# Loading w_out two rows to a partition, with w1, w2 and w3 read in column pairs

## The chip, the cores and the metric

One core of one Trainium2 chip runs the whole program. The metric is the device time of one execution in microseconds, lower being better. The core has five engines that run side by side, each taking its own instructions strictly in its own order: TensorE (matmuls, shown as PE, with its weight loads as PEld), VectorE (DVE), ScalarE (ACT), GpSimd (POOL) and SyncE (SP). Engines wait for each other, and for transfers, by semaphores.

## The reference

The inputs are q, k, v of shape (8, 8, 576, 64), phi of shape (8, 8, 576, 32), three matrices w1, w2, w3 of shape (512, 768), and w_out of shape (768, 512), all float32. Attention goes over 32 memory slots; its result, 4608 tokens of 512 features, goes through a maxout layer:

```python
a = exp(phi - max(phi, axis=2)); a = a / sum(a, axis=2)
k_m = einsum('bhsm,bhsd->bhmd', a, k)
v_m = einsum('bhsm,bhsd->bhmd', a, v)
attn = softmax(q @ k_m.T / sqrt(64))
x = (attn @ v_m).transpose(0, 2, 1, 3).reshape(4608, 512)
h = maximum(maximum(x @ w1, x @ w2), x @ w3)
out = h @ w_out
```

## The kernel before

All matmuls take bfloat16. The kernel never forms x. For each batch it multiplies the values of the memory slots into the weights ("folds" them), so that attention weights times folded weights give the hidden layer directly. The maxout is rewritten: the hidden layer is max(x(w1 - w3), x(w2 - w3), 0) + x w3, and the last term goes past the maximum straight to the output through w3 @ w_out, which is computed once.

The weights lie in SBUF as follows. `w_sb` holds w1, w2 and w3 in one tile: on partition p, for each j of four, row j*128 + p of w1, of w2 and of w3, each with 768 columns. `w12` is a view of it with the 1536 columns of w1 and w2 in one row. `wo_sb` holds w_out, six rows of 512 columns on each partition. `w3T` holds w3 transposed, and `w3o` the product w3 @ w_out.

The order of the work is written out by hand, as a string of short names in `kernel`'s list at the end, and no scheduler changes it. Each name issues one step for one batch (`D1@0` is step D1 for batch 0). What the framework adds are the semaphore waits: it records which addresses each instruction reads and writes, and lets the later of two that overlap wait for the earlier. The steps that matter here:

- `Y2`, `Y3`, `Y0`, `Y1` (in this order) load w3, w_out, w1 and w2 on POOL's queue, with a cast from float32 to bfloat16 on the way (`load_w`, L118, and `load_wo`, L125). The loads of k, v, phi and q (L99, L95, L112) go on the same queue, and are served in its order.
- `W0@0` to `W2@0` transpose w3 on TensorE: 24 transposes of 128 x 128 (`w3_t`, L202), which VectorE copies into `w3T` (L194). `O0@0` to `O3@0` multiply by w_out (`w3_o`, L225). `Z` steps are matmuls on zeros to keep TensorE running (L168).
- `D0` to `D4` are folds (`fold`, L494): matmuls of the 64-row, 32-column form, eight side by side, with 512 or 256 columns of w1 or w2 streaming through. For batch 0 w3 has not been subtracted yet, so the fold runs a second pass with w3 and negated values (`kvtn`). There `D1` has columns 512 to 768 of `w12` (the end of w1), `D0` columns 0 to 512 (w1), `D2` columns 768 to 1024 and `D4` columns 1024 to 1536 (both w2). In later batches `D0`, `D1`, `D2` take 512 columns each. `D3` folds `w3o`.
- `V0@0`, `V1@0`, `V2@0`, `V4@0` subtract w3 from the same column ranges of `w12`, in place, on VectorE (`w_diff`, L244), after the folds of batch 0 have read them.
- `F0` to `F11` are the hidden layer (`ffn1`, L520), even ones with w1 and odd ones with w2; ScalarE and VectorE take the results out of PSUM (L188, L192, L533). `P`, `p` and `T` form the output (L582, L567, L623), which SP stores.
- `S` is the attention score (L387), whose moving operand is every second bfloat16 of the transposed q (`Q`, L367).

Around the change the order by hand reads, for batch 0: `... R1 W0 Y3 W1 W2 H1 H3 Y0 Z6 O0 X1 X0 Y1 O1 L1@1 B1 N1 L0@1 O2 L3@1 K1 L2@1 O3 D1 D0 D3 F10 F8 V0 F4 V1 F0 F6 L2@2 F2 D2 V2 D4 L1@2 p1 L0@2 F3 F1 F11 ...`. A name on one engine does not hold up another engine's names, save through a semaphore.

Of the kernel before, what the change touches and what calls it, by code (L numbers as in the profile page):

```python
# [15 lines left out]
def kernel(  # L16
# [12 lines left out]
    nc = tc.nc  # L29
# [3 lines left out]
    P = 128  # L33
# [38 lines left out]
    w_sb = const.tile([P, NP, 3, DF], BF16, name="w_sb")  # L72
    w3T = const.tile([P, FT, NP, P], BF16, name="w3T")
    wo_sb = const.tile([P, FT, DM], BF16, name="wo_sb")
# [47 lines left out]
    ident = const.tile([P, P], BF16, name="ident")  # L122

    def load_wo():
        nc.gpsimd.dma_start(out=wo_sb, in_=moe_w_out.rearrange("(t p) c -> p t c", p=P))  # L125

    gate = const.tile([1, 2], BF16, name="gate")

# [28 lines left out]
    def one_bank():  # L157
        return psum[:, int(next(banks))]

    def two_banks():  # L160
        i = int(next(banks))
        return psum[:, i : i + 2]
# [12 lines left out]
    def evacuate(kind, n, how, out_, in_, relu=False):  # L175

        swap = "!" in how
        if "^" in how:
            first = "" if EVAC[kind][n] == "a" else "!"
            second = "!" if EVAC[kind][n] == "a" else ""  # L180
            x = 1 if kind == "D" and swap else 0
            evacuate(kind, n, first, out_[:, x], in_[:, x], relu)
            evacuate(kind, n, second, out_[:, 1 - x], in_[:, 1 - x], relu)
            return

        if (EVAC[kind][n] == "a") != swap:
            if relu:
                nc.scalar.activation(out=out_, in_=in_, func=AF.Relu)  # L188
            else:
                nc.scalar.copy(out=out_, in_=in_)  # L190
        elif relu:
            nc.vector.tensor_scalar_max(out=out_, in0=in_, scalar1=0.0)  # L192
        else:
            nc.vector.tensor_copy(out=out_, in_=in_)  # L194

    def w3_t(f2, swap):

        pt = one_bank().bitcast(BF16).rearrange("p (i j n) -> p i j n", i=2, j=NP)
        for i in range(2):
            f = 2 * f2 + i  # L200
            for j in range(NP):
                nc.tensor.transpose(  # L202
                    pt[:, i, j, :], w_sb[:, j, 2, f * P : (f + 1) * P], ident
                )
        evacuate("W", f2, swap, w3T[:, 2 * f2 : 2 * f2 + 2], pt)

# [31 lines left out]
    def columns(b, n):  # L238
        return FIRST[n] if b == 0 else (n * BANK, (n + 1) * BANK)
# [238 lines left out]
    def fold(b, n, swap):  # L478

        s = st[b]  # L480
        lo, hi = (0, DM) if n == 3 else columns(b, n)
        if n == 3:
            wp3s[b] = quad.tile([P, NG, DM], BF16, name="wp3")
        elif b not in wps:
            wps[b] = work.tile([P, NG, 2 * DF], BF16, name="wp")
        ps = two_banks()
        terms = [(s["kvt"][:, 0], w3o[:, :, lo:hi] if n == 3 else w12[:, :, lo:hi])]
        if b == 0 and n != 3:
            terms.append((s["kvtn"], w_sb[:, :, 2, lo % DF : lo % DF + hi - lo]))
        for i, (lhs, rhs) in enumerate(terms):  # L490
            for j in range(NP):
                for a in range(NG):
                    r = slice(HP * a, HP * (a + 1))
                    nc.tensor.matmul(  # L494
                        ps[M * j : M * (j + 1), a, 0 : hi - lo],
                        lhsT=lhs[r, M * j : M * (j + 1)],
                        rhs=rhs[r, j, :],
                        start=(i == 0),
                        stop=(i == len(terms) - 1),
                        tile_position=(HP * a, M * j),  # L500
                    )
        evacuate(
            "D", n, swap, wp3s[b] if n == 3 else wps[b][:, :, lo:hi], ps[:, :, 0 : hi - lo]
        )
# [141 lines left out]
    def issue(b, n, swap):  # L646
# [3 lines left out]
            "I": lambda: [make_identity(nc, ident)]  # L650
            + [nc.gpsimd.memset(x[:, :, :, 2 * D : 2 * D + 1], 1.0) for x in kvrs],
            "Y": lambda: load_w(i) if i < 3 else load_wo(),
            "L": lambda: load_ph(b) if i == 0 else load_q(b) if i == 3 else load_kv(b, i - 1),
            "H": lambda: load_kv(b, i % 2, halves[i // 2]),
# [13 lines left out]
            "M": lambda: ones_sum(b, i),  # L668
            "R": lambda: ones_rec(b, i),
            "D": lambda: fold(b, i, swap),  # L670
            "F": lambda: ffn1(b, i, swap),
            "P": lambda: ffn2_hidden(b, i, range(HEAD)),
            "p": lambda: ffn2_slots(b, i),
            "J": lambda: w3_o_head(i),
            "T": lambda: ffn2(b, i, swap),
            "W": lambda: w3_t(i, swap),
            "O": lambda: w3_o(i, swap),
            "V": lambda: w_diff(i),
# [5 lines left out]
    for w in """  # L684
# [24 lines left out]
        n, b = w.rstrip("!^").split("@")  # L709
# [31 lines left out]
```

## Time and profile before

| | us |
|---|---|
| median of 3 runs | 162.5 (162.21 to 162.69) |
| the profiled execution | 162.81 |
| its span, first to last instruction | 161.0 |
| TensorE busy | 153.0 (95%) |
| VectorE busy | 114.0 (71%) |
| ScalarE busy | 97.0 (60%) |
| GpSimd busy | 81.8 (51%) |

The span is what the profile's timeline covers; the rest of the time lies around it. A busy time is a share of the whole span, over stages with different limits: what one stage waits for is read from the waits and the timeline of that stage. In the lines of a timeline the columns are the start in us, the time taken, the engine, the line of the kernel, the operation, what it writes and reads, and how many such instructions are merged; in brackets is the idle time before, and what ended it. TensorE's granted clock is listed as 1.00 in all slices.

### The profile page before, as it was taken

How to read it: one execution, taken by the hardware profiler on the slowest of the kernel's cores; microseconds unless marked ns; L12 is line 12 of the kernel's file. 1: busy time of each engine (PE TensorE's matmuls, PEld its weight loads, DVE VectorE, ACT ScalarE, POOL GpSimd, SP SyncE). 2: the span in 40 equal slices, each digit the busy share in tenths (PEclk: the TensorE clock that was granted, in tenths of full speed). 3: DMA queues.
4: the chain of work that ended last, by engine and by line, in shares of the span. 5: the costliest groups of instructions: out<-in, count | busy, mean ns of one | idle time of the engine just before them, and what ended most of it. 6: DMA issues, size and time to landing. Idle time of an engine off the chain costs nothing.

```text
span 161.0 us, 4939 instructions
## 1 busy us (share of the span) xinstructions
PE 153.0 (95%) x2062; PEld 85.1 (53%) x2062; DVE 114.0 (71%) x222; ACT 97.0 (60%) x179; POOL 81.8 (51%) x120
## 2 busy tenths in 40 slices
PE   7997799998999999999999999999999999999992
PEld 2442444664467445754674447567553367753451
DVE  2023455998889956887795898999898969771441
ACT  3305413932686769877997998688769895501000
POOL 7275124100599869379939999764908250000000
PEclk9999999999999999999999999999999999999999
DMA  5999999999999999999999999999811430003543
GB/s 152 167 202 207 202 210 210 248 240 212 227 313 254 285 243 263 261 266 226 261 301 245 208 313 296 212 214 253 205 69 40 159 128 7 0 0 133 169 157 132
DMA packets 21991, 31.77 MB, mean 197 GB/s; under 512 B 1233, under 2 KB 16593, under 8 KB 21969
## 3 DMA queue, kind: packets, MB, share of 16 engines
q0 software_dynamic: 16080, 21.43, 70.1%
q1 hardware_dynamic: 5744, 9.90, 17.9%
q8 instruction: 16, 0.26, 0.6%
q10 hardware_dynamic: 144, 0.13, 0.2%
q14 instruction: 7, 0.05, 0.1%
HBM read 39.32 MB, written 9.44 MB: 303 GB/s over the span
## 4 chain that ended last, share of the span: by engine, by line
PE 71%; DMA 21%; POOL 4%; DVE 1%; issue 1%; ACT 0%; POOLq 0%
PE psum L582 26%; PE psum L520 26%; DMA qq<-in_q_dram 13%; PE psum L567 8%; DMA w_sb<-in_moe_w_dram 7%; PE psum L494 4%; PE psum L280 3%; PE psum L387 2%; POOL kvo L99 1%; PE psum L558 1%; POOL t L463 1%; DVE qT L367 1%; PE psum L623 1%; POOL qq L112 0%; DVE attn L471 0%
## 5 line engine op out<-in xcount | busy, mean ns | idle before, releaser
L582 PE MATMUL psum<-wo_sb,hT 128*128 128x512 bf16 x210 | 51.3, 380 | 0.0
L520 PE MATMUL psum<-attn,wp 128*128 128x288 bf16 x384 | 50.3, 287 | 0.2 <-DVE attn L471 0.2
L520 PEld LDWEIGHTS <-wp 128*128 128x128 bf16 x384 | 37.1, 98 | 13.4 <-issue 1.3
L533 DVE TENSOR_TENSOR hT<-psum,h 128x576 bf16<-128x576 f32 x48 | 33.8, 746 | 4.9 <-PE psum L520 2.4
L582 PEld LDWEIGHTS <-hT 128*128 128x128 bf16 x210 | 19.1, 98 | 24.0 <-issue 4.6
L190 ACT CAST wp<-psum 128x1024 bf16<-128x1024 f32 (+2 forms) x33 | 26.5, 860 | 6.5 <-PE psum L494 6.5
L188 ACT ACTIVATE h<-psum 128x576 bf16<-128x576 f32 (+1 forms) x41 | 23.0, 598 | 6.7 <-PE psum L520 5.2
L105 POOL COPY kvr<-kvo 128x2304 bf16<-128x2304 bf16 x12 | 25.3, 2110 | 0.3
L344 POOL COPY kvt<-kvm 32x96 bf16<-32x96 bf16 x48 | 12.4, 259 | 14.1 <-DVE kvm L335 6.7
L463 POOL TENSOR_TENSOR t<-t,sm 128x576 bf16<-128x576 bf16 x14 | 16.0, 1155 | 6.7 <-DVE sm L458 6.4
L567 PE MATMUL psum<-wp,attn 128*128 128x512 bf16 x62 | 18.1, 380 | 0.0
L194 DVE COPY ot<-psum 128x512 f32<-128x512 f32 x15 | 10.2, 677 | 9.9 <-PE psum L567 5.8
L190 ACT COPY ot<-psum 128x512 f32<-128x512 f32 x20 | 11.7, 592 | 8.6 <-PE psum L567 6.0
L99 POOL DMA_DIRECT2D kvo<-in_v_dram x9 | 6.6, 740 | 17.0 <-PE psum L280 13.6
L344 ACT COPY kvt<-kvm 32x96 bf16<-32x96 bf16 x48 | 12.9, 268 | 2.0 <-DVE kvm L335 1.2
L168 PE MATMUL psum<-warm 128*128 128x512 bf16 x44 | 12.6, 442 | 1.2 <-DVE warm L137 1.2
L367 DVE STREAM_TRANSPOSE qT<-qq 128x576 f32<-128x576 f32 x16 | 11.7, 750 | 1.7 <-DMA qq<-in_q_dram 1.7
L396 ACT ACTIVATE e<-psum 128x576 bf16<-128x576 f32 x16 | 9.5, 650 | 5.1 <-PE psum L387 5.0
L260 ACT ACTIVATE e<-ph 128x1152 bf16<-128x1152 f32 (+1 forms) x9 | 9.5, 1057 | 4.3 <-DMA ph<-in_phi_dram 4.2
L441 DVE STREAM_TRANSPOSE t<-e 128x288 f32<-128x288 f32 x14 | 6.6, 470 | 5.6 <-ACT e L396 5.5
L449 DVE TENSOR_REDUCE sm<-t 128x18 f32<-128x576 bf16 x14 | 10.3, 739 | 0.2
L192 DVE TENSOR_SCALAR h<-psum 128x288 bf16<-128x288 f32 (+1 forms) x17 | 9.4, 574 | 0.8 <-ACT ot L190 0.4
(62 smaller groups left out, 137.6 us busy)
## 6 DMA issues: line engine op xcount, KB each, us to landing
out_dram<-ot SPq DMA_DIRECT2D x34, 256.0 KB, 5.8
qq<-in_q_dram POOLq DMA_DIRECT2D x8, 576.0 KB, 13.7
kvo<-in_k_dram POOLq DMA_DIRECT2D x7, 576.0 KB, 15.9
ph<-in_phi_dram POOLq DMA_DIRECT2D x7, 576.0 KB, 14.2
kvo<-in_v_dram POOLq DMA_DIRECT2D x7, 576.0 KB, 18.2
w_sb<-in_moe_w_dram POOLq DMA_DIRECT2D x3, 768.0 KB, 15.0
wo_sb<-in_moe_w_out_dram POOLq DMA_DIRECT2D x1, 768.0 KB, 10.7
ph<-in_phi_dram SPq DMA_DIRECT2D x2, 288.0 KB, 3.3
```

What stands on the lines that cost most here:

```text
L105: nc.gpsimd.tensor_copy(out=kvrs[b % 2][:, :, :, D * i : D * (i + 1)], in_=kvos[b % 2][:, 1 - i])
L168: nc.tensor.matmul(po[:, 0:BANK], lhsT=warm[:, 0:P], rhs=warm, start=True, stop=True)
L188: nc.scalar.activation(out=out_, in_=in_, func=AF.Relu)
L190: nc.scalar.copy(out=out_, in_=in_)
L344: move(out=kvt[R * x : R * (x + 1), :, r], in_=kvm[r, x])
L367: nc.vector.transpose(out=s["qT"][:, j].rearrange("p j c r e -> p (j c r e)").bitcast(FP32), in_=loaded[b]["q"][:, j].rearrange("p j c d - ...
L449: nc.vector.tensor_reduce(out=sm, in_=s["t", g].rearrange("p n r e -> p n e r"), op=ALU.add, axis=mybir.AxisListType.X,)
L463: nc.gpsimd.tensor_tensor(out=t, in0=t, in1=s["sm", g].unsqueeze(2).to_broadcast([P, S // HP, R, 2]), op=ALU.mult,)
L520: nc.tensor.matmul(acc[:, h, 0:SH], lhsT=wps[b][:, g, w * DF + ft * P : w * DF + (ft + 1) * P], rhs=attn[:, g, c0 : c0 + SH], start=(g == ...
L533: nc.vector.tensor_tensor(out=hT[:, ft, (b % 2) * S : (b % 2 + 1) * S].rearrange("p (h n) -> p h n", h=2), in0=a, in1=s["h1", ft], op=ALU.max,
L567: nc.tensor.matmul(po, lhsT=attn[:, g, c0 : c0 + P], rhs=wp3s[b][:, g, :], start=(g == 0 and not done), stop=(last and g == NG - 1),)
L582: nc.tensor.matmul(po, lhsT=hT[:, fc, c0 : c0 + P], rhs=wo_sb[:, fc, :], start=(n == ns[0] and not done), stop=(last and n == ns[-1]),)
```

## The change

w_out's 768 rows were spread so that partition p holds rows p, 128 + p, 256 + p and so on, each row a piece of 512 float32 at its source. Now partition p holds rows 2p and 2p + 1 of each block of 256, so that two neighbouring rows are one piece of 1024 float32. The order of the hidden features in `wo_sb` changes by that, so all that meets it takes the same order: in each block of 256 hidden features, first the 128 even ones, then the 128 odd ones. The folds read the columns of w1, w2 and w3 in that order, with a step of two (`pairs`), and so do the transposes of w3. `D3`, which folds `w3o`, stays as it was, as do the subtractions `V`, which work in place.

```diff
     def load_wo():
-        nc.gpsimd.dma_start(out=wo_sb, in_=moe_w_out.rearrange("(t p) c -> p t c", p=P))
+        nc.gpsimd.dma_start(
+            out=wo_sb.rearrange("p (t e) c -> p t (e c)", e=2),
+            in_=moe_w_out.rearrange("(t p e) c -> p t (e c)", p=P, e=2),
+        )
...
+    def pairs(x):
+
+        return x.rearrange("p (t q e) -> p t e q", q=P, e=2)
+
     def w3_t(f2, swap):
...
                 nc.tensor.transpose(
-                    pt[:, i, j, :], w_sb[:, j, 2, f * P : (f + 1) * P], ident
+                    pt[:, i, j, :], pairs(w_sb[:, j, 2, 2 * f2 * P : 2 * (f2 + 1) * P])[:, 0, i], ident
                 )
...
                         lhsT=lhs[r, M * j : M * (j + 1)],
-                        rhs=rhs[r, j, :],
+                        rhs=rhs[r, j, :] if n == 3 else pairs(rhs[r, j, :]),
```

The lines after `load_wo` move down by three, and those after `w3_t` begins by seven: L494 becomes L501, L520 becomes L527.

## The prediction

> **What bounds the kernel now.** I read the page first, then what TensorE waited for, then the timeline of the stage that the change touches.
>
> ```profile
> span 161.0 us, 4939 instructions
> PE 153.0 (95%) x2062; PEld 85.1 (53%) x2062; DVE 114.0 (71%) x222; ACT 97.0 (60%) x179; POOL 81.8 (51%) x120
> ```
>
> TensorE is busy for 95% of the span. Its waits, in microseconds in all, times, and the longest:
>
> ```profile
> PE psum L225 <- DMA wo_sb<-in_moe_w_out_dram: 1.1, 1, 1.1
> PE psum L387 <- DVE qT L367: 0.8, 2, 0.6
> ...
> PE psum L494 <- DMA w_sb<-in_moe_w_dram: 0.4, 1, 0.4
> ...
> PE psum L520 <- DVE attn L471: 0.2, 1, 0.2
> ```
>
> All of these end by 45.8 us. After that TensorE waits for nothing, so whatever it is late by at 46 us, it is late by at the end. Before that it waits for loads. POOL's queue issues them (start, duration):
>
> ```profile
> 9.20 0.82 POOL L125 DMA_DIRECT2D wo_sb<-in_moe_w_out_dram  x1
> 10.02 1.43 POOL L99 DMA_DIRECT2D kvo<-in_v_dram  x2
> 11.42 1.54 POOL L118 DMA_DIRECT2D w_sb<-in_moe_w_dram  x2
> ```
>
> The last line is w1 and then w2. The three w_sb loads (w3, w1, w2) took from issue to landing:
>
> ```profile
> DMA to landing us min/median/max: 11.8/15.0/18.1
> ```
>
> The queue is served in order, so w1 landed at 11.42 + 15.0 = 26.4 us, and w2, issued at about 12.2, at 12.2 + 18.1 = 30.3 us. Now the first batch's folds and what follows:
>
> ```profile
> 26.59 0.30 PE L494 MATMUL psum<-w_sb,kvt 64*32 64x256 bf16 x8 [0.36 <-DMA w_sb<-in_moe_w_dram]
> ...
> 28.73 1.22 DVE L244 TENSOR_TENSOR w_sb<-w_sb 128x2048 bf16<-128x2048 bf16 x1
> 29.87 0.75 DVE L192 TENSOR_SCALAR h<-psum 128x576 bf16<-128x576 f32 x1
> 30.53 0.68 DVE L244 TENSOR_TENSOR w_sb<-w_sb 128x1024 bf16<-128x1024 bf16 x1
> ...
> 30.63 0.30 PE L494 MATMUL psum<-w_sb,kvt 64*32 64x256 bf16 x8
> ...
> 30.85 0.40 PE L494 MATMUL psum<-w_sb,kvt 64*32 64x512 bf16 x8
> ...
> 31.80 0.68 DVE L244 TENSOR_TENSOR w_sb<-w_sb 128x1024 bf16<-128x1024 bf16 x1
> ```
>
> The reader is to see three things. D1@0 (26.59) starts as soon as w1 is there. D2@0 (30.63), the first user of w2, comes just after w2's landing, with six ffn1 groups of TensorE work between. D4@0 (30.85) follows D2@0 at once, while VectorE is still at V1@0 (30.53 to 31.21) and has not begun V2@0 (31.80 to 32.48).
>
> **The change, part by part.**
>
> *Waits.* The framework writes every semaphore wait from the tiles' address ranges. Comparing the instruction lists of the two built programs, each engine has the same instructions in the same order, but the strided reads of w_sb have other waits. In the changed program (rows of its lists; the remarks in brackets are mine):
>
> ```
> POOL  17 L118 DMACopy w_sb<-in_moe_w1_dram [waits PE]      (none before)
> PE   556 L501 Matmult psum<-w_sb,kvt 32x256 [waits DMASW0] (third matmul of D1@0; none before)
> PE   679 L501 Ldweights kvt [waits DVE]                    (start of D2@0; before: DMASW0)
> PE   712 L501 Matmult psum<-w_sb,kvt 32x512 [waits DVE]    (start of D4@0; before too, for an earlier count)
> ```
>
> By the counts, these are: the load of w1 waits for the w3 transposes, up to the last but one (W2@0); D1@0 waits for the landing of *w2*, of which it reads nothing; D2@0 waits for V1@0; D4@0 waits for V2@0. None is needed by the data. The pattern fits a tracker that takes a strided read to touch all that lies between the first and last address of the other access. No wait of any later fold differs.
>
> 1. *D1@0 waits for w2.* Before, TensorE resumed 26.59 - 26.42 = 0.17 after w1's landing; now it resumes 0.17 after w2's, 30.3 + 0.17 = 30.47. TensorE takes its instructions in order, so D0@0, D3@0 and all ffn1 work of batch 0 queue behind; nothing covers this. Against 26.59 that is +3.88.
>
> 2. *The load of w_out* goes from 768 packets to 384 of twice the size. Between 15.5 and 16.5 us, where only w_out flows, the DMA view counts 201 packets of 1024 B; between 22.5 and 24.5, where only w1/w2 flow, 277 packets of 1536 B. Per packet and DMA engine that is 16 / 201 = 79.6 ns and 16 x 2 / 277 = 115.5 ns; the straight line gives 151 ns at 2048 B. Before 48 x 79.6 = 3.82 us, after 24 x 151 = 3.63: 0.19 sooner for w_out and for all queued behind it, w1 and w2 too. Bounds: at w1's bytes per second (210 against 205 GB/s) 0.09; by the packets' own recorded times (98 and 135 ns, so 172) 48 x 98 - 24 x 172 = 0.58. A loss is left out because packets move more bytes per second the larger they are. I take 0.2, the nearest rows being those of the full queue. TensorE's 1.15 us wait for w_out at 20.04 shrinks by it, and all of that goes into the longer wait of point 1: 3.88 - 0.2 = **+3.7** at D1@0.
>
> 3. *The load of w1 waits for the transposes.* They ran from 16.09 to about 17.5, so POOL issues w1 at 17.6, not 11.42; queued behind it on POOL are w2, k, phi, q and v of the next batch, issued 0.75 apart, the last at 22. In the packet records, w1's first packet starts at 20.65, when the loads ahead of it drain; the very first load of this queue needed 2.5 us from issue (1.25) to first packet (3.76). 17.6 + 2.5 = 20.1 is still ahead of 20.65 - 0.2, so the queue doesn't run dry: I take 0. The margin is 0.35.
>
> 4. *The strided weight loads of the 24 transposes.* The trace has no strided weight load. From below 0; from above each could take twice its 98 ns, 2.4 us in all. The transposes would then end near 19.9, six warm-up matmuls and the late w_out cover TensorE, but w1's issue would move to 20.0 and the queue would stand dry for about 2.0: +2.0 at D1@0. I take 0, as the 128-column load (98 ns) costs hardly more than a 32-column one (88 ns).
>
> 5. *The strided moving reads of the folds.* The score matmuls already read every second bf16, four streams to a partition, as the folds now will:
>
> ```profile
> 39.52 0.48 PE L387 MATMUL psum<-qT,kvt 32*32 32x288 bf16 x32 [0.61 <-DVE qT L367]
> 39.94 0.82 PE L582 MATMUL psum<-wo_sb,hT 128*128 128x512 bf16 x3
> ...
> 43.11 0.84 PE L494 MATMUL psum<-w_sb,kvt 64*32 64x512 bf16 x24
> 43.88 1.47 PE L582 MATMUL psum<-wo_sb,hT 128*128 128x512 bf16 x6
> ```
>
> Two strided passes of 288 columns take 39.94 - 39.52 = 0.42 up to the next group, three contiguous ones of 512 take 0.77. At an equal rate, one line through both gives 0.36 ns a column and 0.21 us fixed. At half rate (0.73 ns) the score's 576 columns would fill all of its 0.42 and leave nothing for the fixed part. So stride 2 runs at full rate: 0. The upper bound is rival C.
>
> 6. *D2@0 waits for V1@0, D4@0 for V2@0.* VectorE's chain moves with TensorE, so in times of before: D2@0 starts at 31.21 + 0.06 = 31.27, not 30.63. It ends near 31.7, before V2@0's turn on VectorE (31.80, after an h at 31.13 that takes 0.75). V2@0 ends at 32.48, D4@0 starts at 32.54, not 30.85: **+1.7**. The rest of batch 0's ffn1 is behind it. Nothing covers it: TensorE has no other instruction before D4@0.
>
> 7. *What is taken back.* S@1 waited 0.61 for q of batch 1, whose landing at 38.0 is now early. What is late next is VectorE: it was free at 37.63, waited 0.41 for q and then took 1.45. It now starts 3.7 + 1.7 = 5.4 later than 37.63 without that wait: **-0.4**. The 0.2 at 45.8 hangs on work that follows S@1 and moves along.
>
> Sum: 3.7 + 1.7 - 0.4 = +5.0. The profiled execution took 162.81 us (161.0 of span and 1.8 around it), 0.3 above the median of 162.5 of the runs shown. So 167.8 for a run like the profiled one, **167.4** as the median.
>
> **Rivals.**
>
> *A, the clock drops in the gap.* TensorE would stand still from about 26.5 to 30.3, far longer than any wait of the trace (1.2). At the program's start the 25 warm-up matmuls took 7.86 us, where later ones of the same shape go at some 0.22 each: 25 x 0.22 = 5.5, so a cold start costs 2.4, though the granted clock is listed as 1.00 in every slice. If the gap brings that state back, the cost falls on the folds and ffn1; about 0.3 is hidden in the waits of point 6, which leaves +2.1: 169.5. For it: the length of the gap. Against it: no drop is visible after the trace's own gaps, though none is as long. [...]
>
> *B, not slower: the load alone counts.* The added waits are met anyway, as most of the waits in the lists are, and w_out's 0.2 (to 0.6) remains: 162.3 (161.9). It decides if w2 lands before D1@0 is ready, by 26.6. Against it: w2 landed at 30.3, and 0.6 at most is gained.
>
> *C, folds at half rate.* A fold pass streams 512 columns in some 0.21; 21 passes for batches 1 to 7 and six for batch 0 at twice that are 27 x 0.21 = +5.7: 173. Against it: point 5; for it: the folds' pattern has two more dimensions.
>
> *D, the packets stay as they are.* If the DMA cuts the 4 KB source rows again, point 2 gives nothing: 167.6.
>
> **How the numbers follow.** Forecast 0.73, D 0.05 (inside the forecast's range), A 0.15, C 0.04, B 0.03. The forecast's own range is 166.7 to 168.4: w_out's 0.58 at the lower end with a few tenths less in point 6, and 0.9 of a dry queue at the upper. Taking in A and most of point 4's upper bound, 166.6 to 169.7. About 0.3% (0.5 us) is what a measurement of this kernel can tell from no change: slower by more has all but B, 0.97; B is split between faster, 0.01, and the same, 0.02.
>
> **What would show it.** In the changed kernel's profile TensorE's longest wait is at L501 for the DMA of w_sb, near 3.7 us ending near 30.3; L501 has waits for VectorE's L251 of 0.6 and 1.1; the w1 load is issued after 17 us on POOL; the packets under 2 KB fall by 768. L225's wait for w_out drops below 1.1. Fold matmuls near 380 ns support point 5; a mean much above 287 ns for L527 (ffn1's matmuls) after 30 us is rival A. It is wrong if D1@0 starts near 26.5.

## The result, and the profile after

The changed kernel takes 169.39 us (median of 4 runs, 168.80 to 170.24) beside 162.38 for the kernel before in the same comparison (162.21 to 162.69): a ratio of 1.0436, 95% interval 1.0405 to 1.0467. It is slower by about 7 us. Its profiled execution took 170.24 us, the longest of the four. The page of the changed kernel, its span, busy times and TensorE's granted clock over 40 slices of 4.2 us:

```profile
span 168.5 us, 4939 instructions
PE 155.5 (92%) x2062; PEld 86.0 (51%) x2062; DVE 114.1 (68%) x222; ACT 97.1 (58%) x179; POOL 81.8 (49%) x120
...
PEclk9999998579999999999999999999999999999999
```

The counts are those of before. VectorE, ScalarE and GpSimd do the same work within 0.1 us; TensorE is busy 2.5 us longer, and its granted clock, 1.00 in every slice before, falls to about half in the eighth slice (29.5 to 33.7 us). So 7.5 us of span are 2.5 of slower matmuls and 5.0 of standing still. Its waits (us in all, times, longest):

```profile
PE psum L501 <- DMA w_sb<-in_moe_w_dram: 4.9, 2, 4.5
PE psum L171 <- DVE warm L140: 1.2, 1, 1.2
PE psum L501 <- DVE w_sb L251: 1.0, 1, 1.0
PE psum L232 <- DMA wo_sb<-in_moe_w_out_dram: 1.0, 1, 1.0
...
PE psum L394 <- DVE qT L374: 0.2, 1, 0.2
```

New are 4.5 us at the folds (L501) for a load of w_sb and 1.0 us for the subtraction V (L251). The wait of 0.6 for q's transpose ahead of S@1 (L394) is gone; the 0.2 listed is batch 0's, at 13.22. Where the new waits fall, in TensorE's timeline of the changed kernel:

```profile
26.07 0.29 PE L501 MATMUL psum<-w_sb,kvt 64*32 64x256 bf16 x2 [0.36 <-DMA w_sb<-in_moe_w_dram]
30.87 0.41 PE L501 MATMUL psum<-w_sb,kvt 64*32 64x256 bf16 x6 [4.52 <-DMA w_sb<-in_moe_w_dram]
...
32.70 4.43 PE L527 MATMUL psum<-attn,wp 128*128 128x288 bf16 x24
37.18 0.31 PE L501 MATMUL psum<-w_sb,kvt 64*32 64x256 bf16 x8
...
38.65 0.42 PE L501 MATMUL psum<-w_sb,kvt 64*32 64x512 bf16 x8 [1.05 <-DVE w_sb L251]
```

D1@0 breaks in two. Two of its matmuls run when w1 lands (26.07); the third, the one with the added wait, stands until 30.87. The six ffn1 groups behind it (24 matmuls) take 4.43 us where they took 3.11. D4@0 waits 1.05 more. The loads, from the same kernel's timeline of POOL, and the time from issue to landing of the three w_sb loads:

```profile
17.40 1.50 POOL L118 DMA_DIRECT2D w_sb<-in_moe_w_dram  x2 [6.20 <-PE psum L209]
```

```profile
DMA to landing us min/median/max: 8.5/11.3/12.7
```

w1 and w2 are issued at 17.40 and some 18.15, after a wait of 6.20 for the w3 transposes (L209); before, w1 was issued at 11.42. w1 lands at 17.40 + 8.5 = 25.9, w2 at 18.15 + 12.7 = 30.85: the first is when D1@0 begins, the second when it goes on. The clock in three stretches of 5 us (columns: the stretch, its length, busy time and instructions of PE, PEld, DVE, ACT and POOL, granted clock, DMA share, GB/s):

```profile
26.00:31.00 5.00, 0.42 (x10) 0.25 (x18) 0.44 (x1) 0.00 (x0) 0.75 (x1) 0.76 1.18 218
31.00:36.00 5.00, 5.00 (x55) 2.92 (x45) 3.07 (x5) 2.75 (x5) 0.74 (x1) 0.56 1.16 255
36.00:41.00 5.00, 3.90 (x55) 2.32 (x53) 3.06 (x5) 3.41 (x5) 0.00 (x0) 1.00 1.22 210
```

In the first stretch TensorE is busy for 0.42 us of 5, and VectorE and ScalarE, which take its results, hardly more; in the second it is busy throughout, at a granted clock of 0.56. In the trace's clock records it is 0.50 from 28.6 to 35.4 us, 6.83 us in all.

### The profile page after: what moved, and what is told of

Read it like the earlier page. It is cut to its first block, busy times and chain, and to the rows that moved or that the text cites. A ratio compares the mean times of both kernels' runs of the same rounds, so it can differ in the third digit from the quotient of the medians.

```text
span 168.5 us, 4939 instructions
## 1 busy us (share of the span) xinstructions
PE 155.5 (92%) x2062; PEld 86.0 (51%) x2062; DVE 114.1 (68%) x222; ACT 97.1 (58%) x179; POOL 81.8 (49%) x120
## 2 busy tenths in 40 slices
DMA packets 21606, 31.77 MB, mean 189 GB/s; under 512 B 1232, under 2 KB 15824, under 8 KB 21584
## 4 chain that ended last, share of the span: by engine, by line
PE 76%; DMA 14%; POOL 4%; DVE 2%; issue 1%; ACT 0%; POOLq 0%; DVEq 0%
PE psum L527 29%; PE psum L589 25%; DMA w_sb<-in_moe_w_dram 14%; PE psum L574 8%; PE psum L501 5%; PE psum L287 3%; PE psum L394 2%; POOL kvo L99 1%; PE psum L565 1%; POOL t L470 1%; PE psum L209 1%; DVE qT L374 1%; PE psum L630 1%; POOL qq L112 0%; DVE hT L540 0%
## 5 line engine op out<-in xcount | busy, mean ns | idle before, releaser
L527 PE MATMUL psum<-attn,wp 128*128 128x288 bf16 x384 | 51.5, 291 | 0.2 <-DVE attn L478 0.2
L527 PEld LDWEIGHTS <-wp 128*128 128x128 bf16 x384 | 37.8, 99 | 14.4 <-issue 1.3
L540 DVE TENSOR_TENSOR hT<-psum,h 128x576 bf16<-128x576 f32 x48 | 33.7, 745 | 6.6 <-PE psum L527 2.4
L193 ACT CAST wp<-psum 128x1024 bf16<-128x1024 f32 (+2 forms) x33 | 26.6, 859 | 13.3 <-PE psum L501 13.3
L501 PE MATMUL psum<-w_sb,kvt 64*32 64x512 bf16 (+1 forms) x200 | 9.0, 393 | 6.0 <-DMA w_sb<-in_moe_w_dram 4.9
L171 PE MATMUL psum<-warm 128*128 128x512 bf16 x44 | 12.1, 427 | 1.2 <-DVE warm L140 1.2
L197 DVE CAST wp<-psum 128x512 bf16<-128x512 f32 (+1 forms) x11 | 6.9, 637 | 5.8 <-PE psum L501 5.8
```

Of the source, the lines that this page charges most:

```text
L501: nc.tensor.matmul(ps[M * j : M * (j + 1), a, 0 : hi - lo], lhsT=lhs[r, M * j : M * (j + 1)], rhs=rhs[r, j, :] if n == 3 else pairs(rhs[r, ...
L527: nc.tensor.matmul(acc[:, h, 0:SH], lhsT=wps[b][:, g, w * DF + ft * P : w * DF + (ft + 1) * P], rhs=attn[:, g, c0 : c0 + SH], start=(g == ...
L540: nc.vector.tensor_tensor(out=hT[:, ft, (b % 2) * S : (b % 2 + 1) * S].rearrange("p (h n) -> p h n", h=2), in0=a, in1=s["h1", ft], op=ALU.max,
```

## The experiments

The theory to be tested: the waits that the strided reads bring are the whole loss, through three parts (the wait for w2, the clock after it, the waits for V), and the paired load, the strided reads themselves and w1's late issue cost nothing. Its rivals: one of these last three costs something itself. Kernels of one group below ran on the same chip beside the kernel before; ratios are to that. All edits are to the changed kernel, unless the text says otherwise.

**Group 1.** `load_only` keeps the paired load and undoes all strided reads, so w_out's rows meet the wrong hidden features:

```diff
-                    pt[:, i, j, :], pairs(w_sb[:, j, 2, 2 * f2 * P : 2 * (f2 + 1) * P])[:, 0, i], ident
+                    pt[:, i, j, :], w_sb[:, j, 2, f * P : (f + 1) * P], ident
...
-                        rhs=rhs[r, j, :] if n == 3 else pairs(rhs[r, j, :]),
+                        rhs=rhs[r, j, :],
```

> The kernel before with the paired load of w_out alone; the folds and the transposes of w3 read as before, so the rows of w_out meet the wrong hidden features and the output is not the reference's. Theory (the added waits cost the time, the load helps a little): 162.2 us, between 161.8 and 162.4; w_out's packets are 384 of 2048 B, TensorE's wait for w_out falls from 1.1 to about 0.9 us, no wait above 1.2. Rival (the larger pieces delay w2 and so cost part of the 7 us): 163 or more, with w2 landing after 30.5.

Measured: 162.29 us (12 runs), ratio 0.9999 (0.9980 to 1.0018). The load by itself brings nothing that can be measured, at most 0.3 us. Its wait for w_out, in TensorE's waits of this kernel, is that of before:

```profile
PE psum L228 <- DMA wo_sb<-in_moe_w_out_dram: 1.1, 1, 1.1
```

`no_false_waits` was to keep every part of the change and lose only the waits. w3 gets a tile of its own. Batch 0's folds read w1 and w2 in plain order, and the copy out of PSUM into `wp` makes the pair order:

```diff
-    w_sb = const.tile([P, NP, 3, DF], BF16, name="w_sb")
+    w_sb = const.tile([P, NP, 2, DF], BF16, name="w_sb")
+    w3_sb = const.tile([P, NP, DF], BF16, name="w3_sb")
...
-                        rhs=rhs[r, j, :] if n == 3 else pairs(rhs[r, j, :]),
+                        rhs=rhs[r, j, :] if n == 3 or b == 0 else pairs(rhs[r, j, :]),
...
+        if b == 0 and n != 3:
+            to = to.rearrange("p g (t e q) -> p g t q e", q=P, e=2)
+            of = of.rearrange("p g (t q e) -> p g t q e", q=P, e=2)
+        evacuate("D", n, swap, to, of)
```

> The changed kernel with w3 in a tile of its own, and with batch 0's folds of w1 and w2 reading their columns in plain order, the order being made in the copy out of PSUM. All engines then have the waits of the kernel before. Load, transposes and the folds of seven batches stay paired. Theory: 162.4, between 162.0 and 162.9 (-0.2 from the load, +0.2 from the folds, whose groups of 24 took 0.80 instead of 0.77 us in the changed kernel's trace), granted clock 1.00, no wait above 1.2 us. Rival (the strided reads themselves are slow): 164 or more, with the fold matmuls of the later batches well above 390 ns.

Measured: 171.87 us, ratio 1.0593 (1.0559 to 1.0626). It failed as a test, because of its own copies. The rows of the tile `wp` between 24 and 36 us show them (duration least, median, longest):

```profile
L194 ACT CAST wp<-psum x5: 938/2433/5033, 26.6 to 34.7; 128x512 bf16<-128x512 f32 x3, 128x256 bf16<-128x256 f32 x1, 128x1024 bf16<-128x1024 f32 x1
L198 DVE CAST wp<-psum x3: 886/1290/2636, 26.7 to 29.9; 128x512 bf16<-128x512 f32 x2, 128x256 bf16<-128x256 f32 x1
```

They write neighbouring values 256 bytes apart, and take up to 5.0 us, where the same copies took at most 1.02 in the kernel before; TensorE waits 6.7 us for them. Nothing follows for the theory.

`own_w3` takes only the new tile for w3 from it (the first three lines of that diff, and its uses). The load of w1 then has no wait for the transposes, and the folds keep theirs.

> The changed kernel with w3 in a tile of its own: the load of w1 no longer waits for the transposes, the three waits of batch 0's folds stay. Theory (the folds' waits carry the loss): 169, between 168.3 and 169.7; w1 issued near 11.4, D1@0 still waits 3.7 to 4.5 us for w2, the clock still at 0.50 for some 6.8 us. Rival (the late issue of w1 makes the gap so long that the clock drops): w2 lands 0.6 sooner, the wait is 3.7, the clock stays at 1.00, 167.

Measured: 168.82 us, ratio 1.0403 (1.0363 to 1.0444), its interval overlapping the changed kernel's 1.0405 to 1.0467. w1 is issued at 10.99, about as early as in the kernel before, and the folds wait as in the changed kernel. TensorE's waits of this kernel:

```profile
PE psum L502 <- DMA w_sb<-in_moe_w_dram: 4.0, 2, 3.6
...
PE psum L502 <- DVE w_sb L252: 1.2, 1, 1.2
```

The clock was at 0.50 for 6.83 us here too. So the loss is not w1's late issue.

`first_plain` takes the other half: one tile for the weights, plain folds in batch 0 with the same copies, so that of the added waits only w1's stays.

> The changed kernel with batch 0's folds of w1 and w2 in plain order and the copies out of PSUM making the pairs: the folds' waits are those of before, and only the load of w1 still waits for the transposes (issued near 17.4). Theory: 162.5, between 162.1 and 163.1; the queue never runs dry. Rival (the late issue costs on its own): 163.5 to 165, with w1 or w2 landing later than in the kernel before (26.4 and 30.3).

Measured: 172.44 us, ratio 1.0607 (1.0575 to 1.0639). The copies cover everything again (6.7 us of waits for them). Inconclusive in time; the trace does show that D1@0 waits 0.4 for its load, as in the kernel before, although w1 was issued at 18.69 in it.

**Group 2.** `no_false_waits2` turns the copies around: they read PSUM with a step of two and write without one.

```diff
+        if n != 3 and b == 0:
+            to = to.rearrange("p g (t e q) -> p g t e q", q=P, e=2)
+            of = of.rearrange("p g (t q e) -> p g t e q", q=P, e=2)
```

> As no_false_waits, but the copies of batch 0 out of PSUM read PSUM with a step of two and write SBUF in one run, where before they wrote SBUF with a step of 256 bytes and took up to 5.0 us each. Theory (waits alone cost the time; the first version was slow by its copies): the copies take 0.4 to 1.1 us, 162.4, between 162.0 and 163.0, clock 1.00 throughout. Rival (paired reading of the folds or the transposes costs on its own): 164 or more with no long wait at the folds of batch 0.

Measured: 162.37 us (12 runs) beside 162.27, ratio 1.0002 (0.9986 to 1.0018). The copies take 0.37 to 1.02 us, as those of the kernel before do. TensorE's largest waits of this kernel hold nothing for V and, at the folds, the 0.4 for w_sb of before:

```profile
PE psum L172 <- DVE warm L141: 1.2, 1, 1.2
PE psum L233 <- DMA wo_sb<-in_moe_w_out_dram: 1.1, 1, 1.1
PE psum L210 <- DMA w_sb<-in_moe_w_dram: 1.1, 1, 1.1
PE psum L360 <- DVE kvn L331: 0.4, 1, 0.4
PE psum L502 <- DMA w_sb<-in_moe_w_dram: 0.4, 1, 0.4
```

This kernel has the paired load, the strided transposes and strided folds in seven batches of eight, and costs what the kernel before costs. The whole loss is the added waits. It also says that the change without them gains nothing.

`w2_wait_only` and `v_waits_only` divide the loss. Both have w3 in its own tile and these copies; the first has D2@0 and D4@0 plain, so that only D1@0's wait for w2 is left, the second D0@0 and D1@0, so that only the waits for V are:

```diff
+                        rhs=rhs[r, j, :] if n == 3 or (b, n) in ((0, 2), (0, 4)) else pairs(rhs[r, j, :]),
...
+                        rhs=rhs[r, j, :] if n == 3 or (b, n) in ((0, 0), (0, 1)) else pairs(rhs[r, j, :]),
```

> As own_w3, but D2@0 and D4@0 read in plain order (copies reading PSUM with a step of two), so that only D1@0's wait for w2 is left of the added waits. Theory: 167.5, between 166.9 and 168.2: the gap of 3.6 us and the 6.8 us of half clock stay, the 1.2 us before D4@0 go. Rival (the wait for VectorE merely follows from the late start and the rest is hidden anyway): 168.8, as own_w3.

Measured: 167.59 us, ratio 1.0355 (1.0311 to 1.0399). TensorE's timeline of this kernel:

```profile
29.92 0.41 PE L502 MATMUL psum<-w_sb,kvt 64*32 64x256 bf16 x6 [3.41 <-DMA w_sb<-in_moe_w_dram]
...
31.75 3.65 PE L531 MATMUL psum<-attn,wp 128*128 128x288 bf16 x24
35.33 0.30 PE L502 MATMUL psum<-w_sb,kvt 64*32 64x256 bf16 x8
```

The wait is 3.41 us, the clock records show 0.50 for 3.41 us (29.46 to 32.88), and the 24 ffn1 matmuls take 3.65, between 3.11 and 4.43. This wait alone makes most of the loss.

> As own_w3, but D1@0 and D0@0 read in plain order, so that only D2@0's and D4@0's waits for the subtractions V1@0 and V2@0 are left. Theory: 163.7, between 163.1 and 164.2: 1.7 us of waits for VectorE on L502-like lines less the 0.4 taken back before the scores of batch 1; clock 1.00. Rival (with TensorE on time the waits are hidden): 162.4.

Measured: 163.92 us, ratio 1.0104 (1.0078 to 1.0130). TensorE's timeline of this kernel shows both waits, at full clock (by medians the two parts are 5.3 and 1.65 us, together the 7.0 of the changed kernel):

```profile
31.02 0.31 PE L502 MATMUL psum<-w_sb,kvt 64*32 64x256 bf16 x8 [0.57 <-DVE w_sb L252]
...
32.28 0.42 PE L502 MATMUL psum<-w_sb,kvt 64*32 64x512 bf16 x8 [0.84 <-DVE w_sb L252]
```

`warm_in_gap` tests the clock: 20 warm-up matmuls ahead of D1@0 fill the gap. (The list of PSUM banks gets one more entry for the added step, here and in the kernels below; it is not shown.)

```diff
-        L1@1 B1@0 N1@0 L0@1 O2@0! L3@1 K1@0! L2@1 O3@0! D1@0^ D0@0^ D3@0^ F10@0 F8@0 V0@0 F4@0!
+        L1@1 B1@0 N1@0 L0@1 O2@0! L3@1 K1@0! L2@1 O3@0! Z20@0 D1@0^ D0@0^ D3@0^ F10@0 F8@0 V0@0 F4@0!
```

> The changed kernel with 20 more warm-up matmuls (512 columns of zeros, some 4.3 us) just ahead of D1@0, where TensorE stands waiting for w2. Theory (rival A of the prediction is real, and 2.0 of the loss is the clock): granted clock 1.00 in every slice, L527's matmuls 286 ns throughout, 167.4, between 166.8 and 168.0, which was the forecast without a drop of the clock. Rival (the half clock is hidden in the waits for VectorE): 169.0 to 169.6.

Measured: 169.47 us, ratio 1.0443 (1.0415 to 1.0470): no gain in the time. Yet the clock stayed at 1.00, and S@1 started at 44.89 instead of 46.86. Most of the 2.0 gained was lost behind it: 5.37 late against before at S@1, it was 6.93 late at the end of the span. For 1.08 of these 1.56, TensorE's timeline of this kernel shows

```profile
48.24 0.23 PE L287 MATMUL psum<-kvo,e 64*32 64x64 bf16 x9 [1.08 <-issue]
```

a stall in which it waited for nothing that the trace shows. The changed kernel has no such line. As the edit's 40 instructions (20 matmuls, 20 weight loads) are all that was added, the next kernels add none.

**Groups 3 and 4.** `warm_moved` takes 12 of the 25 warm-up matmuls at the start and puts them into the gap, so that the number of instructions stays.

```diff
-        E@0 H0@0 H2@0 L3@0 Z25@0 B0@0 I@0 N0@0 Z2@0 K0@0! Q0@0 Q1@0 Z9@0 S@0 Z2@0 M0@0 M1@0
+        E@0 H0@0 H2@0 L3@0 Z13@0 B0@0 I@0 N0@0 Z2@0 K0@0! Q0@0 Q1@0 Z9@0 S@0 Z2@0 M0@0 M1@0
...
+        L1@1 B1@0 N1@0 L0@1 O2@0! L3@1 K1@0! L2@1 O3@0! Z12@0 D1@0^ D0@0^ D3@0^ F10@0 F8@0 V0@0 F4@0!
```

> The changed kernel with 12 of the 25 warm-up matmuls at the program's start moved just ahead of D1@0, so that no instruction is added after D1@0's place and the gap splits into 2.6 us of work and less than 3 us of standing still. Theory (the drop of the clock costs 2.0 us; in warm_in_gap it was saved up to batch 1's scores, at 5.4 us instead of 7.3 behind the kernel before, and then lost again in 1.6 us of stalls that belong to the 40 added instructions): clock 1.00, no stall of 1 us at L287, 167.4, between 166.9 and 167.9. Rival (what the clock gives is taken back by other waits): 169.0 to 169.6.

> The changed kernel once more, for its spread beside warm_moved. Theory: 168.8 to 170.3 with the clock at 0.50 for one or two stretches of 3.4 us near 28 to 36 us in the profiled run; D1@0 waits 3.5 to 4.5 us.

Measured: `warm_moved` 168.28 us, ratio 1.0366 (1.0345 to 1.0387); the changed kernel again, on the same chip, 169.44, ratio 1.0443 (1.0408 to 1.0478). The intervals are apart, but 168.28 lies above the 166.9 to 167.9 expected: by medians 1.2 us are gained. The profiled execution of the second took 171.53, far above its median, so only its clock records and the gap ahead of them are used. TensorE's timeline of `warm_moved`:

```profile
26.40 2.75 PE L171 MATMUL psum<-warm 128*128 128x512 bf16 x12
29.09 0.29 PE L501 MATMUL psum<-w_sb,kvt 64*32 64x256 bf16 x2
30.92 0.30 PE L501 MATMUL psum<-w_sb,kvt 64*32 64x256 bf16 x6 [1.55 <-DMA w_sb<-in_moe_w_dram]
...
31.94 3.11 PE L527 MATMUL psum<-attn,wp 128*128 128x288 bf16 x24
```

D1@0 goes on at the same time as in the changed kernel (30.92 beside 30.87), since w2 decides that, but with at most 1.55 of idle time ahead, and the ffn1 groups take their 3.11 again. The clock drop is a cost of its own.

The kernel has another one at its start, where the 12 matmuls were taken away. The clock on its page, and TensorE's timeline there:

```profile
PEclk9969999999999999999999999999999999999999
...
7.67 0.24 PE L287 MATMUL psum<-kvo,e 64*32 64x128 bf16 x4 [0.89 <-DMA kvo<-in_k_dram]
9.01 0.76 PE L287 MATMUL psum<-kvo,e 64*32 64x128 bf16 x68 [1.11 <-DMA kvo<-in_k_dram]
...
10.89 3.32 PE L171 MATMUL psum<-warm 128*128 128x512 bf16 x9
```

The clock records show 0.50 from 9.92 to 13.33 us, and the nine matmuls at 10.89 take 3.32 us where before they took 2.11, though no idle stretch just ahead is longer than 1.11 us. This lies ahead of the stage that is compared here.

The last two runs ask whether w1's late issue counts once the clock is out of the way. `warm_moved2` is `warm_moved` once more on another chip; `own_w3_warm` adds the new tile for w3 to it, so that w1 is issued at 10.79.

> warm_moved with w3 in a tile of its own, so that w1 is issued near 11.4 and not near 17.5 us; D1@0's wait for w2 and the waits for VectorE stay, and the clock is held in the gap. Theory A (the late issue of w1 alone delays w2's landing, by 0.6 to 1.0 us on its last DMA engines): 167.5, between 167.1 and 167.8, D1@0 resumes near 30.0. Theory B (the late issue is harmless, the landings scatter by themselves): as warm_moved, 168.1 to 168.5.

> warm_moved once more, as the other half of the pair: 168.1 to 168.5 by either theory.

Measured: `own_w3_warm` 167.83 us, ratio 1.0321 (1.0285 to 1.0358); `warm_moved2` 167.75, ratio 1.0317 (1.0283 to 1.0351), below the 168.1 to 168.5 expected of it. No difference between the two: the late issue costs nothing that can be measured. The clock stayed at 1.00 in the gap in both. w2 landed 0.6 earlier in the profile of the first, but single landings scatter as much between runs of one kernel (D1@0 went on at 30.44 in one `warm_moved` profile and at 30.92 in the other). No version tried is faster than the kernel before.

## Why the prediction was right, and where it was off

The direction, the cause and the range (166.6 to 169.7) were right; the likeliest time, 167.4, is 2.0 below the 169.39 measured, and the forecast's own range, 166.7 to 168.4, was missed: the wider one held because it took in rival A, which came in. For a run like the profiled one, 167.8 was forecast and 170.24 measured; of these 2.4, point 1 below has 0.6 and the clock 1.8. From TensorE's timelines, the loss up to S@1 in four terms: when D1@0 goes on, and the time from there to D2@0, on to D4@0, and on to S@1 (us):

| kernel | D1@0 goes on | to D2@0 | to D4@0 | to S@1 | S@1 | against before |
|---|---|---|---|---|---|---|
| before | 26.59 | 4.04 | 0.22 | 8.67 | 39.52 | |
| after | 30.87 | 6.31 | 1.47 | 8.21 | 46.86 | +7.34 |
| own_w3 | 30.22 | 6.54 | 1.59 | 8.20 | 46.55 | +7.03 |
| w2_wait_only | 29.92 | 5.41 | 0.23 | 8.17 | 43.73 | +4.21 |
| v_waits_only | 26.34 | 4.68 | 1.26 | 8.20 | 40.48 | +0.96 |
| warm_moved | 30.92 | 4.70 | 1.26 | 8.20 | 45.08 | +5.56 |
| warm_moved2 | 30.44 | 4.71 | 1.27 | 8.20 | 44.62 | +5.10 |
| no_false_waits2 | 26.84 | 4.04 | 0.22 | 8.18 | 39.28 | -0.24 |

In `after`, 7.34 at S@1 are 7.4 at the end of the span: what TensorE is late by there stays. The table sets single profiled executions side by side, and each can lie about 1 us off the median of its kernel.

*Point 1, the wait for w2: right, and 0.6 too small.* Forecast +3.7, measured +4.28 (30.87 - 26.59). The other kernels with this wait, `own_w3_warm` and `warm_in_gap` among them, went on between 29.80 and 30.92, +3.2 to +4.3, around the forecast (31.60 in the long execution of `after_again`). Why w2 lands about 1 us later in some runs than in others stays open.

*Point 2, the load of w_out: a gain too small to show.* Packets under 2 KB fell from 16593 to 15824, 769 fewer, so D is out. The new ones take 173 ns at the median, the 172 that the prediction drew from the recorded times; in a stretch of 1 us with little else the queue carried 207 GB/s with them (`load_only`), 205 without (before). The 0.2 is not excluded by the interval of `load_only`, nor shown.

*Point 3, w1's late issue: right.* It was issued at 17.40 (forecast 17.6), its first packet started at 20.13 (before 20.65): the queue was not dry.

*Point 4, strided weight loads: right.* Their 24 in the transposes take 97 to 100 ns in `after`, the contiguous ones 96 to 100 before.

*Point 5, strided moving reads: right within 0.2 us.* The folds of the form 64x512 that stream w_sb past `kvt` take 388 ns in the mean in `no_false_waits2`, 381 before, and the three folds of a later batch, 24 matmuls in one group, 0.87 - 0.84 = 0.03 us more, some 0.2 for seven batches. C, at half rate, is out.

*Point 6, the waits for V: right.* Forecast +1.7. With the clock at full speed, in `v_waits_only`, D2@0 comes 4.68 - 4.04 = 0.64 later and D4@0 another 1.26 - 0.22 = 1.04: 1.68. In `after` only D4@0's shows as a wait (1.05); D2@0's does not, since the slow ffn1 groups end together with V1@0, at 37.13, and D2@0 starts at 37.18.

*Point 7, what is taken back: the size came out, the reason is not shown.* Forecast -0.4; in the profiles it is 8.21 - 8.67 = -0.46. But `load_only` and `no_false_waits2`, which aren't late at D1@0, have no wait for q ahead of S@1 either, and `v_waits_only` is 1.65 slower by medians, which is all of point 6 with nothing taken back. So the 0.61 may belong to the one profiled execution of the kernel before, and be part of the 0.3 by which that lies above the median; then the prediction took it off twice. This stays open.

*The step that failed* is the weighing of rival A, which had 0.15 beside 0.73 for the forecast. The argument was that "no drop is visible after the trace's own gaps, though none is as long": gaps of 1.2 us say nothing of one of 3.7. The gap did bring the drop, and its size was nearly right: forecast +2.1, and after minus `warm_moved` gives (6.31 - 4.70) + (1.47 - 1.26) = 1.8 in the profiles (1.2 by medians). In part that is luck: the price was taken from the program's start, where the 25 matmuls took 7.86 us in the profile of before, but 7.29 in that of `after`, 2.4 and 1.8 above 5.5. With the clock held, the change comes to 1.0317 to 1.0366, some 167.5 to 168.3 on a base of 162.38, beside a forecast of 166.7 to 168.4 without the drop. A's own time was 169.5. In the traces the clock fell to 0.50 in each of the four in which the wait for w2 was left open (3.41 us in `w2_wait_only`, 3.58 in `own_w3`, 4.52 in `after`, 4.56 in `after_again`), and stayed at 1.00 in the four where warm-up matmuls stood in it (longest wait left 0.57 in `warm_in_gap`, 1.49 in `warm_moved2`, 1.55 in `warm_moved`, 1.71 in `own_w3_warm`).

*Rival B* is out: the added waits did cost time, as w2 landed at 30.85 in `after`, not by 26.6.

That the framework's tracker takes a strided read for all that lies in its span is inferred from the lists of waits; shown is that a tile of its own for w3 frees w1's load, that plain reads in batch 0 free the folds, and that with both the loss is gone.

## What to carry to other kernels

After a change of an access pattern, compare the waits that the framework writes, and not only the instructions: here the same 4939 instructions took 7 us more, through waits that no data asked for. A tile of its own, or contiguous reads while the loads are under way, takes such waits off. The open gaps on TensorE here (3.41 to 4.56 us) were paid twice, as the gap and, by the table, as some 1.4 to 2.2 us of slow matmuls behind it (`w2_wait_only`, `after`, `own_w3`); with warm-up matmuls in the gap the ffn1 groups took their 3.11 again. In `warm_moved`, which took these from the program's start, the clock was at 0.50 there, from 9.92 to 13.33 us.

## What the runs showed of the hardware

**The clock in and behind the gap.** In the traces' clock records TensorE's granted clock stood at 0.50 for 3.41 us in `w2_wait_only`, and for 6.83 us in `after`, `own_w3` and `after_again`. The drop came 2.0 us after TensorE's last matmul ahead of the wait in `own_w3`, 2.3 in `after`, 3.0 in `w2_wait_only` and 3.4 in `after_again`: not in the order of the gaps (3.58, 4.52, 3.41 and 4.56 us). A drop also came where no single wait was as long: in `warm_moved` at 9.92 us, for 3.41 us, behind idle stretches of 0.89 and 1.11 us. Over the span of that profile the mean granted clock was 0.990; in `warm_moved2`, with waits of 2.4 and 1.1 us at the start, 0.990 too, and in `own_w3_warm`, with 1.5 and 1.1, 0.997. By the table above, the gap's shorter drop cost some 1.4 us (5.41 - 4.04, `w2_wait_only`), the longer 1.8 to 2.2 (`after` and `own_w3` beside `warm_moved`). Of the four runs of the changed kernel, the one of 170.24 us had a mean granted clock of 0.980, those of 168.80 to 169.76 of 0.988 to 0.990; before, at 162.21 to 162.69, the profiled one had 1.000. What sets the start and the length of a drop is not shown here.

**The copies that make the pairs.** Copies of 256 to 1024 float32 a partition from PSUM to bfloat16 took 0.9 to 5.0 us where they wrote with a step of 256 bytes, and 0.37 to 1.02 where they read PSUM with a step of two instead, the same as with no step in the kernel before (0.37 to 1.02).

**A stall without a known cause.** With twenty matmuls added in the gap (`warm_in_gap`) TensorE stood for 1.08 us some 17 us behind the last of them, and the trace names no cause. The changed kernel and `warm_moved`, which add no instructions, have no such stall; that the added instructions bring it was not tried by itself.
